# A Fourier filter and a two-layer network on one core: how the array between the two forward stages is laid out in DRAM, which loads come first, and one step more between a piece and its inverse pair

## The chip, the core and the metric

The kernel runs on one core of a Trainium2 chip. Its engines work side by side and wait for each other by semaphores: TensorE (PE in the profile; its weight loads are PEld) multiplies matrices, VectorE (DVE) and ScalarE (ACT) do element-wise work and empty the matrix accumulators in PSUM, GpSimd (POOL) and SyncE (SP) here mainly issue DMAs. [...] The metric is the device time of one execution in microseconds. Before the change three runs took 862.39, 861.15 and 859.33 us, median 861.15 us.

## The reference

```python
def _attn_ref(x, filt_r, filt_i):               # x: 8 x 3008 x 256
    X = np.fft.rfft(x, axis=1)
    F = (filt_r + 1j * filt_i)[None, :, :]      # 1505 x 256
    y = np.fft.irfft(X * F, n=x.shape[1], axis=1)
    return y.astype(np.float32)

def _moe_ref(x, w_in, w_out, alpha):            # x: 24064 x 256, w_in: 256 x 2048
    h = x @ w_in
    g = np.maximum(h, 0.0) + alpha * np.minimum(h, 0.0)
    return (g @ w_out).astype(np.float32)       # w_out: 2048 x 256
```

The first function's result, its 8 x 3008 rows taken as 24064 tokens, goes into the second. Arrays come and go in float32; the kernel works in fp16 with float32 accumulation.

## The kernel before

**The transform.** 3008 is 47 times 64. Each of the eight batches goes through four stages of small matrix products, called pieces here; a class `Fft` holds one batch.

- Stage A (`piece_a`, L162, 16 pieces): the 47-point transform. A piece is one product of 94 x 512 (L168) into a PSUM bank named psF, copied to `asb` by L250 (ACT) or L253 (DVE). Rows of `asb` are 96 = two halves h times 48 numbers k; along a row lie 32 values of s, each with 256 channels. `save_a` (L171) writes a quarter of `asb` to `a_dram`, after every fourth piece.
- `turn_a` (L175) reads `a_dram` back as `at`, with s on the partitions: the turn between the two forward stages. It can begin only when all four saves have landed.
- Stage B (`piece_b`, L184, 12 pieces): two products L188 into psF, then two DVE multiplications with the filter, uu (L191, by `filt_s`) and ww (L192, by `filts_s`). Batch 0 uses `piece_b0` (L195), with other banks.
- Stage C (`piece_c`, L211, 12 inverse pairs): four products, L220 (reads uu) and L221 (reads ww), into psF, copied to `v` by ACT. `turn_c` (L224) writes `v` to `v_dram` by quarters and, after the last, reads `v_dram` back as `zt` by quarters. Each read starts when the writes have landed.
- Stage D (`piece_d`, L238, 16 pieces): four small products L243 into psF, copied to `yT`, the input of the network.

**The network.** 48 blocks of tokens (`sizes`, L300: twelve for each pair of batches, the sixth of 384 tokens, the others of 512), of 16 steps each. Step j runs `up(j)` (L327): two products L332 into the bank pair `hps`; at an odd j the activation follows, ACT `gt` (L337), DVE `m` twice (L340) and an addition (L341). Then comes `down(j)` (L344) of the block before: four (three) products L350 into `op`, and at j = 7 and 15 (10 and 15 in a short one) a copy `osb` (L355, ACT) and its stores (L316).

**The order.** Nothing is rearranged by a scheduler: each engine executes its instructions as the Python code issues them. The prologue runs batch 0 through A, B and C and four D pieces. Then the steps are counted on, 0 to 767, and `plan` (L359 on) puts the pieces of batch b at given steps: after `up` and `down` of its step, a piece is issued. `plan_fft(b, a0, ga, ta, b0, gap, d0)` puts A piece i at step a0 + ga i, the turn at ta, B piece k at b0 + gap k, its inverse pair (C) three steps after it, and D from d0 on. Block 6 of each pair of batches (step 96 on) needs the D pieces of the odd batch.

**Banks.** psF has two banks for all pieces A, B, C and D. A piece may begin only when the copy (or, for B, the ww product) that empties its bank is done. Which bank a piece gets is decided when the program is built, so not strictly in turn.

**Queues.** SP issues saves, turns, `v_dram` and `zt`, constants and stores, strictly in order; a DMA that must wait holds up all behind it. POOL issues, also in order, what is converted from float32: x (`load_x`, L120, eight DMAs a batch), the filter (`load_filt`, L126), w_in (`win_s`) and w_out (`wout_s`). Each of the two has eight semaphores for its DMAs, so a ninth waits until the first has landed. Two small POOL copies into `gate` hold the queue: the first (L273) until `at` of batch 0 has landed, the second (L293) until `zt` of batch 0 has.

`filts_s`, the filter with its two halves exchanged, is made by two DMAs from `filt_s` (L291), issued after `zt` of batch 0; batch 1 is the first to read it. `xs` has four buffers, so a load of the next batch waits until the A pieces of the buffer's present contents are done.

Of the kernel before, what the change touches and what calls it, by code (L numbers as in the profile page):

```python
# [10 lines left out]
FP16 = mybir.dt.float16  # L11
# [5 lines left out]
NK1 = 24  # L17
D = 256
NB = 8
DFF = 2048  # L20
NH = 32
# [45 lines left out]
def kernel(  # L67
# [10 lines left out]
    nc = tc.nc  # L78
# [4 lines left out]
    twi_d = nc.inline_tensor(twi_np.astype(np.float16), name="c_twi")  # L83

    konst = ctx.enter_context(tc.tile_pool(name="konst", bufs=1))
# [7 lines left out]
    psO = ctx.enter_context(tc.tile_pool(name="psO", bufs=2, space=bass.MemoryType.PSUM))  # L93
    psF = ctx.enter_context(tc.tile_pool(name="psF", bufs=2, space=bass.MemoryType.PSUM))
    dram = ctx.enter_context(tc.tile_pool(name="dram", bufs=1, space=bass.MemoryType.DRAM))
    a_dram = dram.tile([NB, 96, NH, D], FP16, name="a_dram")
    v_dram = dram.tile([NB, 96, NH, D], FP16, name="v_dram")
    ctx.enter_context(tc.manual_schedule())

# [4 lines left out]
    twi_s = konst.tile([128, NK1, 2, 128], FP16, name="twi_s")  # L104
    filt_s = konst.tile([128, NK1, D], FP16, name="filt_s")
# [4 lines left out]
    alm_s = konst.tile([128, 16], FP32, name="alm_s")  # L110
    win_s = konst.tile([128, 2, DFF], FP16, name="win_s")
    wout_s = konst.tile([128, 16, D], FP16, name="wout_s")
    gate = konst.tile([128, 2], FP16, name="gate")
    yT = konst.tile([128, 2, 2 * NFFT], FP16, name="yT")

    def xrow(b, h, c):
        return bass.AP(tensor=x.tensor, offset=x.offset + (b * NFFT + NH * h + 8 * c) * D,
                       ap=[[N2 * D, N1], [1, 8 * D]])

    def load_x(b, c):  # L120
        xs = p_x.tile([2 * N1, 8 * D], FP16, name="xs")
        for h in range(2):
            nc.gpsimd.dma_start(out=xs[h * N1 : h * N1 + N1], in_=xrow(b, h, c))  # L123
        return xs

    def load_filt(dst, pbase, src, ka, kb):  # L126
        n = kb - ka
        nc.gpsimd.dma_start(
            out=dst[pbase : pbase + 32, ka:kb],
            in_=bass.AP(tensor=src.tensor, offset=src.offset + ka * D,  # L130
                        ap=[[47 * D, 32], [D, n], [1, D]]))
        nc.gpsimd.dma_start(
            out=dst[pbase + 32 : pbase + 64, ka:kb],
            in_=bass.AP(tensor=src.tensor, offset=src.offset + (N1 - ka) * D,
                        ap=[[47 * D, 32], [-D, n], [1, D]]))

    nc.sync.dma_start(out=wf1_s, in_=wf1_d.ap())
    xc = {(0, c): load_x(0, c) for c in range(4)}
    nc.sync.dma_start(out=al16, in_=moe_alpha.rearrange("(j p) -> j p", p=128))
    nc.sync.dma_start(out=twf_s[:, 0:12], in_=twf_d.ap()[:, 0:12])  # L140
    for ka, kb in ((0, 12), (12, 24)):
        load_filt(filt_s, 0, filt_r, ka, kb)
        load_filt(filt_s, 64, filt_i, ka, kb)
    make_identity(nc, id32)

    def bank(wide=False):
# [5 lines left out]
    class Fft:  # L152
# [16 lines left out]
            evict(self.asb[:, 2 * i : 2 * i + 2].rearrange("p a d -> p (a d)"), ps[0:96])  # L169

        def save_a(self, c):  # L171
            s = slice(8 * c, 8 * c + 8)
            nc.sync.dma_start(out=a_dram[self.b, :, s], in_=self.asb[:, s])

        def turn_a(self, eng, ka=0, kb=NK1):  # L175
            for h in range(2):
                for c in range(2):
                    r = h * 48 + c * NK1
                    q = c * 64 + NH * h
                    eng.dma_start(  # L180
                        out=self.at[q : q + NH, ka:kb],
                        in_=a_dram[self.b, r + ka : r + kb].rearrange("k s d -> s k d"))

        def piece_b(self, kp):  # L184
            px = bank().rearrange("p (k d) -> p k d", k=2)
# [69 lines left out]
    both = (on_act, on_dve)  # L255


    f0 = Fft(0)
# [2 lines left out]
        if i % 4 == 3:  # L261
            f0.save_a(i // 4)
    f0.turn_a(nc.sync, 0, 12)
    f0.turn_a(nc.scalar, 12, 24)
    nc.sync.dma_start(out=twi_s[:, 0:12], in_=twi_d.ap()[:, 0:12])
    nc.sync.dma_start(out=twf_s[:, 12:24], in_=twf_d.ap()[:, 12:24])
    nc.sync.dma_start(out=twi_s[:, 12:24], in_=twi_d.ap()[:, 12:24])
    nc.sync.dma_start(out=wi3_s, in_=wi3_d.ap())
# [1 line left out]
    nc.tensor.transpose(alp[:, 0, 0:16], al16, id32)  # L270
    nc.vector.tensor_copy(al_s, alp[:, 0, 0:16])
    nc.gpsimd.tensor_scalar(alm_s, al_s, 1.0, -1.0, OP.mult, OP.add)
    nc.gpsimd.tensor_copy(gate[:, 0:1], f0.at[:, 11, 0:1])  # L273
    for kt in range(2):
        nc.gpsimd.dma_start(out=win_s[:, kt], in_=moe_w_in[kt * 128 : (kt + 1) * 128])
    for q in range(2):
        nc.gpsimd.dma_start(
            out=wout_s[:, 8 * q : 8 * q + 8],
            in_=moe_w_out[1024 * q : 1024 * q + 1024].rearrange("(j p) d -> p j d", p=128))
# [10 lines left out]
        o = 64 * half  # L290
        nc.sync.dma_start(out=filts_s[o : o + 64], in_=filt_s[64 - o : 128 - o])  # L291

    nc.gpsimd.tensor_copy(gate[0:96, 1:2], f0.zt[:, 31, 0:1])  # L293
    for c in range(4):
        xc[(1, c)] = load_x(1, c)
    for i in range(4):
        f0.piece_d(i, both[i % 2], i % 2 == 1)

# [62 lines left out]
    def put(step, fn, *args):  # L361
        plan.setdefault(step, []).append((fn, args))

    def plan_fft(b, a0, ga, ta, b0, gap, d0):
        f = Fft(b)
        for i in range(16):
            put(a0 + ga * i, f.piece_a, i, on_act)
        for c in range(4):
            put(a0 + ga * (4 * c + 3), f.save_a, c)
            if b + 1 < NB:  # L370
                put(a0 + ga * (4 * c + 3) + 1,
                    lambda b=b, c=c: xc.update({(b + 1, c): load_x(b + 1, c)}))
        put(ta, f.turn_a, nc.sync)
        for kp in range(12):
            put(b0 + gap * kp, f.piece_b, kp)
            put(b0 + gap * kp + 3, f.piece_c, kp, on_act)
        for q in range(4):
            put(b0 + gap * (3 * q + 2) + 4, f.turn_c, q)
        for i in range(16):
            put(d0 + min(i, 4) + 2 * max(i - 4, 0), f.piece_d, i, on_act)  # L380

    for i in range(4, 16):
        put(i - 4, f0.piece_d, i, both[i % 2])
    plan_fft(1, 10, 1, 26, 40, 3, 92)
    plan_fft(2, 50, 2, 86, 104, 5, 187)
    for b in range(3, NB):
        p = 96 * (b - 1)
        plan_fft(b, p - 54, 2, p - 22, p + 6, 5, p + 91)

    prev = None  # L390
    step = 0
# [43 lines left out]
```

## Time and profile before

| What | Value |
|---|---|
| Median of three runs | 861.15 us (859.33 to 862.39) |
| Profiled execution: span | 861.4 us, 0.25 us over the median |
| PE busy | 799.4 us (93%) |
| DVE, ACT busy | 612.9 us (71%), 586.6 us (68%) |
| First A piece, first B piece of batch 0 | 7.5 us, 33.0 us |
| First D piece of batch 0, first `up` | 63.1 us, 64.6 us |
| B pieces of batch 1 begin (step 40) | 110.4 us |
| B pieces of batch 2 begin (step 104) | 186.6 us |
| PE busy from 200 to 680 us | 474.5 of 480 us |

The time that lies around the span is not shown apart: the profiled execution is given by its span alone, and it agrees with the runs to 0.03%.

The page's second part cuts the span into 40 slices of 21.5 us and shows, in tenths, how busy each engine was; its fourth part follows the chain of work that ended last back from the end; the timeline shows instructions in order of time, with the idle time before an instruction and what ended it in square brackets; the stretches view sums busy time by engine in stretches that one names. In the stretches view GB/s is what the DMA engines moved, counted at the writing side, and the DMA share can be over 1, since packets overlap.

### The profile page before, as it was taken

What the parts mean: (1) busy time and instruction counts of PE and PEld (TensorE: products, weight loads), DVE (VectorE), ACT (ScalarE), POOL (GpSimd) and SP (SyncE); (2) the same over time, 40 slices, a digit from 0 to 9 for tenths busy, and PEclk for the clock granted to TensorE, in tenths of its full rate; (3) what the DMA queues carried; (4) which work ended last, traced back from release to release, by engine and by line L of the source; (5) the groups of instructions that cost most, each with busy time, mean ns of one, the idle gap of its engine ahead of it and who ended that gap; (6) DMA issues with size and microseconds to landing.
All of it is one profiled execution on the core that took longest, in us unless ns stands there. A gap on an engine that the chain in (4) does not pass through costs nothing.

```text
span 861.4 us, 15404 instructions
## 1 busy us (share of the span) xinstructions
PE 799.4 (93%) x5809; PEld 541.7 (63%) x5809; DVE 612.9 (71%) x1361; ACT 586.6 (68%) x817; POOL 41.4 (5%) x85
## 2 busy tenths in 40 slices
PE   3458989979999999999999999999999999999997
PEld 1134556756666766676666766676666766676665
DVE  2246668758877787678877787778877788777773
ACT  2027757767787767777777767777777866677663
POOL 4103000000000000000000000000000000000000
PEclk9989989999999999999999999999999999999999
DMA  9989835761368224772268323682148122411111
GB/s 212 250 171 197 179 69 133 157 144 41 75 148 199 60 62 97 172 158 51 53 162 195 73 64 83 164 181 50 43 120 186 50 68 50 129 38 39 39 41 49
DMA packets 95378, 95.95 MB, mean 111 GB/s; under 512 B 8312, under 2 KB 85128, under 8 KB 95176
## 3 DMA queue, kind: packets, MB, share of 16 engines
q1 hardware_dynamic: 85448, 78.19, 35.8%
q0 software_dynamic: 8256, 16.00, 12.3%
q10 hardware_dynamic: 1600, 0.79, 0.5%
q8 instruction: 45, 0.74, 0.4%
q14 instruction: 29, 0.24, 0.1%
HBM read 59.55 MB, written 49.81 MB: 127 GB/s over the span
## 4 chain that ended last, share of the span: by engine, by line
PE 70%; DVE 13%; ACT 7%; DMA 6%; issue 2%; SPq 1%; POOL 0%; ACTq 0%; DVEq 0%; POOLq 0%
PE hps L332 29%; PE op L350 28%; ACT gt L337 6%; DVE gt L341 4%; DVE m L340 4%; PE psF L168 3%; DVE ww L192 3%; DVE uu L191 3%; PE psF L221 2%; DMA at<-a_dram 2%; PE psF L243 2%; DMA a_dram<-asb 2%; PE psF L220 1%; DMA xs<-in_x_dram 1%; PE psF L188 1%
## 5 line engine op out<-in xcount | busy, mean ns | idle before, releaser
L337 ACT ACTIVATE gt<-hps 128x1024 f16<-128x1024 f32 (+1 forms) x384 | 385.1, 1003 | 134.6 <-PE hps L332 134.1
L332 PE MATMUL hps<-yT,win_s 128*128 128x512 f16 (+1 forms) x1536 | 454.3, 377 | 1.1 <-ACT yT L250 1.0
L350 PE MATMUL op<-wout_s,gt 128*128 128x256 f16 x3008 | 453.3, 273 | 0.6 <-DVE gt L341 0.6
L350 PEld LDWEIGHTS <-gt 128*128 128x128 f16 x3008 | 294.4, 98 | 192.5 <-issue 2.8
L340 DVE TENSOR_SCALAR m<-gt,alm_s 128x512 f16<-128x512 f16 (+1 forms) x768 | 233.5, 346 | 164.1 <-ACT gt L337 162.8
L341 DVE TENSOR_TENSOR gt<-gt,m 128x1024 f16<-128x1024 f16 (+1 forms) x384 | 261.6, 681 | 24.3 <-DVE m L340 0.9
L332 PEld LDWEIGHTS <-win_s 128*128 128x128 f16 x1536 | 145.6, 98 | 31.6 <-issue 5.0
L250 ACT ACTIVATE asb<-psF 96x512 f16<-96x512 f32 x120 | 70.7, 593 | 40.2 <-PE psF L168 40.2
L250 ACT ACTIVATE v<-psF 128x512 f16<-128x512 f32 x84 | 50.2, 598 | 34.9 <-PE psF L221 34.9
L250 ACT ACTIVATE yT<-psF 128x376 f16<-128x376 f32 x120 | 58.1, 484 | 20.9 <-PE psF L243 20.7
L191 DVE TENSOR_TENSOR uu<-psF,filt_s 128x512 f16<-128x512 f32 x84 | 57.4, 683 | 6.7 <-PE psF L188 6.7
L355 ACT ACTIVATE osb<-op 128x512 f32<-128x512 f32 x96 | 56.3, 587 | 6.9 <-PE op L350 3.7
L168 PE MATMUL psF<-xs,wf_s 94*96 94x512 f16 x120 | 47.8, 398 | 11.0 <-DMA xs<-in_x_dram 8.3
L192 DVE TENSOR_TENSOR ww<-psF,filts_s 128x512 f16<-128x512 f32 x84 | 57.1, 679 | 0.0
L123 POOL DMA_DIRECT2D xs<-in_x_dram x64 | 32.9, 522 | 458.2 <-PE psF L168 457.1
L243 PE MATMUL psF<-wi_s,zt 96*128 96x94 f16 x504 | 42.7, 207 | 10.8 <-DMA zt<-v_dram 9.0
L243 PEld LDWEIGHTS <-zt 96*128 96x128 f16 x512 | 36.3, 100 | 18.9 <-DMA zt<-v_dram 9.3
L221 PE MATMUL psF<-ww,twi_s 128*128 128x256 f16 x168 | 41.1, 272 | 6.2 <-DVE ww L192 3.5
L220 PE MATMUL psF<-uu,twi_s 128*128 128x256 f16 x168 | 42.9, 272 | 1.1 <-ACT yT L250 0.5
L188 PE MATMUL psF<-at,twf_s 128*128 128x256 f16 x168 | 32.3, 274 | 8.1 <-issue 4.5
L220 PEld LDWEIGHTS <-twi_s 128*128 128x128 f16 x192 | 19.0, 99 | 18.0 <-issue 13.2
L250 ACT ACTIVATE v<-op 128x512 f16<-128x512 f32 x12 | 7.2, 597 | 32.4 <-PE op L221 32.4
(35 smaller groups left out, 130.8 us busy)
## 6 DMA issues: line engine op xcount, KB each, us to landing
out_dram<-osb SPq DMA_DIRECT2D x128, 128.0 KB
a_dram<-asb SPq DMA_DIRECT2D x32, 384.0 KB
v_dram<-v SPq DMA_DIRECT2D x128, 96.0 KB
zt<-v_dram SPq DMA_DIRECT2D x32, 384.0 KB
xs<-in_x_dram POOLq DMA_DIRECT2D x64, 188.0 KB, 5.1
at<-a_dram SPq DMA_DIRECT2D x28, 384.0 KB
twi_s<-c_twi SPq DMA_DIRECT2D x2, 768.0 KB
filts_s<-filt_s SPq DMA_DIRECT2D x2, 768.0 KB
```

The costliest lines, as they stand in the source:

```text
L168: nc.tensor.matmul(ps[0:96], wf1_s, xs[:, o : o + 512], start=True, stop=True)
L191: nc.vector.tensor_mul(uu, px, filt_s[:, 2 * kp : 2 * kp + 2])
L192: nc.vector.tensor_mul(ww, px, filts_s[:, 2 * kp : 2 * kp + 2])
L220: nc.tensor.matmul(pv[:, kh], twi_s[:, k1, 0], uu[:, kh], start=True, stop=False)
L221: nc.tensor.matmul(pv[:, kh], twi_s[:, k1, 1], ww[:, kh], start=False, stop=True)
L243: nc.tensor.matmul(ps[:, m], self.zt[:, 8 * g + 4 * mh + m, dh * 128 : dh * 128 + 128], wi3_s, start=True, stop=True)
L250: nc.scalar.activation(o, i, AF.Copy)
L332: nc.tensor.matmul(self.hps[:, j % 2, 0:tn], win_s[:, kt, j * 128 : (j + 1) * 128], yT[:, kt, self.t0 : self.t0 + tn], start=(kt == 0), st ...
L337: nc.scalar.activation(g[:, :, 0:tn], self.hps[:, :, 0:tn], AF.Copy)
L340: nc.vector.tensor_scalar(m[:, i, 0:tn], g[:, i, 0:tn], 0.0, a, OP.min, OP.mult)
L341: nc.vector.tensor_add(g[:, :, 0:tn], g[:, :, 0:tn], m[:, :, 0:tn])
L350: nc.tensor.matmul(self.op[:, si % 2], self.gts[k][:, 128 * si : 128 * si + 128], wout_s[:, k], start=(k == 0), stop=(k == 15))
```

## The change

Five things are changed.

1. `a_dram` is laid out as s, k, channel in place of k, s, channel. `save_a` writes it in two DMAs (one for each half h), each in pieces of 512 bytes with gaps; `turn_a` reads it in two DMAs (64 partitions each, one for each c) in place of four, each partition's share being contiguous (12 KB; 6 KB in each half of batch 0's turn).
2. In the prologue the first half of `twi_s` is loaded right after the first half of `twf_s`, in place of after the turn; the second half of the filter is loaded after the first `gate`, in place of before it; the second half of batch 0's turn is issued by SP in place of ACT.
3. The x of batch 1 is loaded ahead of w_out; the second `gate` is gone.
4. Batch 1's A pieces lie at steps 2 to 17 in place of 10 to 25 and are emptied by ACT and DVE in turn, in place of ACT alone; its turn is at 20 in place of 26, its B pieces at 32, 36, ... in place of 40, 43, ...; the turns of batches 3 to 7 are two steps later.
5. In all planned batches the inverse pair is four steps after its B piece in place of three, and `turn_c` follows one step later too.

```diff
-    a_dram = dram.tile([NB, 96, NH, D], FP16, name="a_dram")
+    a_dram = dram.tile([NB, 2 * NH, 2 * NK1, D], FP16, name="a_dram")
...
     nc.sync.dma_start(out=twf_s[:, 0:12], in_=twf_d.ap()[:, 0:12])
-    for ka, kb in ((0, 12), (12, 24)):
-        load_filt(filt_s, 0, filt_r, ka, kb)
-        load_filt(filt_s, 64, filt_i, ka, kb)
+    nc.sync.dma_start(out=twi_s[:, 0:12], in_=twi_d.ap()[:, 0:12])
+    load_filt(filt_s, 0, filt_r, 0, 12)
+    load_filt(filt_s, 64, filt_i, 0, 12)
...
         def save_a(self, c):
-            s = slice(8 * c, 8 * c + 8)
-            nc.sync.dma_start(out=a_dram[self.b, :, s], in_=self.asb[:, s])
+            for h in range(2):
+                r = NH * h + 8 * c
+                nc.sync.dma_start(
+                    out=a_dram[self.b, r : r + 8].rearrange("s k d -> k s d"),
+                    in_=self.asb[48 * h : 48 * h + 48, 8 * c : 8 * c + 8])
 
         def turn_a(self, eng, ka=0, kb=NK1):
-            for h in range(2):
-                for c in range(2):
-                    r = h * 48 + c * NK1
-                    q = c * 64 + NH * h
-                    eng.dma_start(
-                        out=self.at[q : q + NH, ka:kb],
-                        in_=a_dram[self.b, r + ka : r + kb].rearrange("k s d -> s k d"))
+            for c in range(2):
+                eng.dma_start(
+                    out=self.at[64 * c : 64 * c + 64, ka:kb],
+                    in_=a_dram[self.b, :, NK1 * c + ka : NK1 * c + kb])
...
     f0.turn_a(nc.sync, 0, 12)
-    f0.turn_a(nc.scalar, 12, 24)
-    nc.sync.dma_start(out=twi_s[:, 0:12], in_=twi_d.ap()[:, 0:12])
+    f0.turn_a(nc.sync, 12, 24)
...
-    nc.gpsimd.tensor_copy(gate[:, 0:1], f0.at[:, 11, 0:1])
+    nc.gpsimd.tensor_copy(gate, f0.at[:, 11, 0:1])
+    load_filt(filt_s, 0, filt_r, 12, 24)
+    load_filt(filt_s, 64, filt_i, 12, 24)
     for kt in range(2):
         nc.gpsimd.dma_start(out=win_s[:, kt], in_=moe_w_in[kt * 128 : (kt + 1) * 128])
+    for c in range(4):
+        xc[(1, c)] = load_x(1, c)
     for q in range(2):
         nc.gpsimd.dma_start(
             out=wout_s[:, 8 * q : 8 * q + 8],
...
-    nc.gpsimd.tensor_copy(gate[0:96, 1:2], f0.zt[:, 31, 0:1])
-    for c in range(4):
-        xc[(1, c)] = load_x(1, c)
...
-    def plan_fft(b, a0, ga, ta, b0, gap, d0):
+    def plan_fft(b, a0, ga, ta, b0, gap, d0, evicts=(on_act, on_act)):
         f = Fft(b)
         for i in range(16):
-            put(a0 + ga * i, f.piece_a, i, on_act)
+            put(a0 + ga * i, f.piece_a, i, evicts[i % 2])
...
-            put(b0 + gap * kp + 3, f.piece_c, kp, on_act)
+            put(b0 + gap * kp + 4, f.piece_c, kp, on_act)
         for q in range(4):
-            put(b0 + gap * (3 * q + 2) + 4, f.turn_c, q)
+            put(b0 + gap * (3 * q + 2) + 5, f.turn_c, q)
...
-    plan_fft(1, 10, 1, 26, 40, 3, 92)
+    plan_fft(1, 2, 1, 20, 32, 4, 92, both)
     plan_fft(2, 50, 2, 86, 104, 5, 187)
     for b in range(3, NB):
         p = 96 * (b - 1)
-        plan_fft(b, p - 54, 2, p - 22, p + 6, 5, p + 91)
+        plan_fft(b, p - 54, 2, p - 20, p + 6, 5, p + 91)
```

More of the change, by code (lines that the diff above doesn't have):

```diff
@@ L112 @@
     wout_s = konst.tile([128, 16, D], FP16, name="wout_s")
-    gate = konst.tile([128, 2], FP16, name="gate")
+    gate = konst.tile([128, 1], FP16, name="gate")
     yT = konst.tile([128, 2, 2 * NFFT], FP16, name="yT")
```

## The prediction

> **What bounds the kernel now.** I read the page's slices first, then stretches, the chain and the timeline of each hole.
>
> ```profile
> PE   3458989979999999999999999999999999999997
> DMA  9989835761368224772268323682148122411111
> ```
>
> From the tenth slice on TensorE is full; what can be won lies before 200 us and in small gaps. The DMA row is near full just where PE is not. Stretches (start and end, length, busy time of PE, PEld, DVE, ACT and POOL, the granted clock, DMA share, GB/s):
>
> ```profile
> 15.80:33.00 17.20, 0.00 (x0) 0.00 (x0) 0.00 (x0) 0.00 (x0) 0.20 (x1) 1.00 1.18 249
> 54.70:63.00 8.30, 0.00 (x0) 0.00 (x0) 0.00 (x0) 0.02 (x1) 0.00 (x0) 0.68 0.68 159
> 105.90:110.30 4.40, 0.00 (x0) 0.00 (x0) 1.07 (x3) 0.22 (x1) 0.00 (x0) 0.84 1.20 214
> 110.30:115.80 5.50, 5.43 (x20) 2.92 (x21) 2.60 (x5) 1.57 (x2) 0.00 (x0) 0.51 0.11 37
> 182.90:186.50 3.60, 0.03 (x1) 0.00 (x0) 1.18 (x3) 0.48 (x1) 0.00 (x0) 1.00 1.02 228
> 186.50:190.90 4.40, 4.35 (x22) 2.56 (x23) 2.60 (x5) 2.37 (x4) 0.00 (x0) 0.61 0.01 4
> ```
>
> Four holes: the turn of batch 0, its way from C to D, the turns of batches 1 and 2. Behind the last two the clock is half for 5.4 and 3.4 us, so each costs half of that again. The chain names the DMAs of the first two:
>
> ```profile
> 15.74 6.18 DMA a_dram<-asb
> 23.40 9.52 DMA at<-a_dram
> 56.08 2.00 DMA v_dram<-v
> 58.20 4.83 DMA zt<-v_dram
> ```
>
> Two places of the timeline carry the rest: a D piece of batch 0 that waits for the DVE copy behind the activation, and an inverse pair that waits for ww.
>
> ```profile
> 71.01 1.02 ACT L337 ACTIVATE gt<-hps 128x1024 f16<-128x1024 f32 x1
> 72.07 0.62 DVE L340 TENSOR_SCALAR m<-gt,alm_s 128x512 f16<-128x512 f16 x2 [0.20 <-ACT gt L337]
> 72.72 0.69 DVE L341 TENSOR_TENSOR gt<-gt,m 128x1024 f16<-128x1024 f16 x1
> 73.33 0.54 DVE L253 CAST yT<-psF 128x376 f16<-128x376 f32 x1
> 73.92 0.33 PE L243 MATMUL psF<-wi_s,zt 96*128 96x94 f16 x4 [0.34 <-DVE yT L253]
> ...
> 217.36 0.68 DVE L192 TENSOR_TENSOR ww<-psF,filts_s 128x512 f16<-128x512 f32 x1
> 217.50 0.27 PE L220 MATMUL psF<-uu,twi_s 128*128 128x256 f16 x1
> 218.09 0.27 PE L221 MATMUL psF<-ww,twi_s 128*128 128x256 f16 x1 [0.32 <-DVE ww L192]
> ```
>
> **Part 1, batch 0 up to its first B piece (33.0 us).** From 2.6 us on the DMA engines are never free, so bytes count. Rates from stretches: x 211 GB/s (6 to 8 us), w_in and w_out 207 (38 to 42), scattered reads of a turn 193 (178 to 184), scattered 512-byte writes of `v_dram` 282 (48 to 50), long contiguous reads 333 to 432 (32 to 36). Ahead of the first B piece there is less: half the filter, 0.79 MB at 143 to 250 GB/s, 4.4 us; half the turn, with the other half now contiguous, 7.2 us (24 to 33 us less latency) become 2.1. There is more: 0.79 MB of `twi_s`, 2.1 us, and the saves' 1.57 MB at 282 GB/s in place of 332 or more (16 to 18 us): 0.9 at least, I take 1.5. Four more SP issues of 0.5 us hide between the A pieces, but the last, which delays the turn. Latency, covered by the queue before, adds 1.5. Sum -4.4 -5.1 +2.1 +1.5 +1.5 = -4.4: first B at about 29 (27.5 to 31; scattered writes as slow as scattered reads give +2.5). The turn's second half, moved from ACT to SP, is issued 1 us later and is needed 12 us later; nothing.
>
> The filter's second half, behind the first gate, must land before B piece 6 (12.6 us after the first: 45.6 against 33.05). Four issues of 0.6 us and 4.4 us of transfer beside 3 us of `twf_s` and `twi_s` put it at 9.5: covered.
>
> **Part 2, from C to D (63.1 us).** Behind the gate POOL now has 0.79 MB of filter, 1.05 of w_in, 1.54 of x, 1.05 of w_out: 4.4 + 5 + 7.3 + 5.2 = 22 us; SP has 2.1 + 2.9 us of turn and constants and 5.6 of `v_dram`. From 29.5 that fills the engines to 61 or 62. Before, all had landed at 50 and the last write and the `zt` read ran alone: 54.7 to 58.1 and 58.2 to 63.0. How long they take beside other loads the trace shows in part: the first quarter of v, beside w_out, took 7.9 us from its first issue at 41.87 to 49.8, the last 3.3. C ends 21.7 us after the first B: 50.7. Then v 3.3 to 7.9, I take 6.8; `zt` 4.8 to 8.5, I take 6.8, since w_out runs out meanwhile. D begins at 64.4 (59 to 68): 1.3 us lost where 4.4 were won.
>
> **Part 3, D and A together.** x of batch 1 is there now: its wait (76.7 us, 0.9) goes. But steps 2 to 11 hold a D and an A piece each. By the program's waits, one psF bank then serves only D, the other only A, and at odd steps both are emptied by DVE, behind m, m and the addition of the same step. Before, a D piece waited for a DVE copy three steps old. Now, from the start of an activation: 1.02 to its end, 0.62 m, 0.69 addition, 0.54 yT, D starts at +2.91 (71.01 to 73.92 above), `asb` 0.69, A starts at +3.55; A, up and ACT's copy of A (0.38 + 0.59) bring the next activation at +4.45. Two steps thus take 4.45 us, where activations stood 2.0 apart (68.76 to 74.72: three pairs in 6.0). Following it through: activation of step 3 at 6.7 after the first D, of step 11 at 24.5, then 8.2 to step 18, at 32.7. With 14 steps of 0.87 step 32 is reached after 45.0 us; before, after 34.8 (97.9 less 63.1), A pieces until step 25 included. Loss 10.2 (6 to 13). PE is busy only 1.6 of 4.45 us; should its clock fall, each pair costs 0.6 more, up to 2.7 in all; I take 0.8, since windows at 60% stayed fast and one at 25% did not.
>
> [...]
>
> **Part 4, the turn of batch 1.** The last save is issued 35.5 to 36.3 us after the first D, lands 2 later; two issues, 1.15 of latency, 1.57 MB at 333 to 432 GB/s: `at` lands at about 44 and is wanted at 45.9. The hole (4.65 by start times) and its slow clock (half of 5.4) go: 7.3 won (4 if x of batch 2 slows the read by 3). `filts_s` (7.4 us behind `zt`) is long there.
>
> **Part 5, B and C of batch 1.** With a gap of four steps C, B and A of batch 2 meet in steps 52 to 76, seven times; A waits 0.63 for the copy of v, as four times before (and 0.34 once): 1.5 lost.
>
> **Part 6, batch 2's turn and batch 1's D.** `turn_c` of the last quarter is at step 81, not 77, and stands on SP behind three stores (2.35 us) and the two saves of step 80. From the start of step 80: stores to 3.7, saves to 4.6, v to 6.5, landed at 8.8, `zt` 4.9 later (163.86 to 168.83 before): 13.7. D is wanted at 10.65. A new wait of 3.1 (1.5 to 5) with 1.6 of slow clock (0 to 1.7). The old hole at step 104 (3.8 and 1.7) is covered, as the turn is issued right behind `zt` and lands 4 us early. Won: 0.8 (-2 to +4).
>
> **Part 7, the inverse pairs.** From batch 2 on, six pairs of a batch start L221 late (0.59 from L220, not 0.11, above) or L220 late: by start times 13.5 us in all, 0.25 to 0.57 each. ww ends 0.5 too late; a step is 0.87, so all go. New waits, from the program's banks: a B behind a D whose copy stands behind gt and osb on ACT (0.43) and an A behind a pair in a step with osb (0.5), in five or six batches: 4.6. Won 8.9 (5 to 11). The two-step shift of later turns costs nothing: they have 26 steps; SP waits less.
>
> [...]
>
> **Sum.** -1.3 -10.2 -0.8 +7.3 -1.5 +0.8 +8.9 = 3.2 us won: 858.2 by the profiled span of 861.4, which is 0.25 over the median; so 858.0.
>
> **Rivals.**
> - The front is early: x and w_out leave `v_dram` and `zt` their old times. For it: `v` at 51 to 54 us ran 3.3 just behind w_out. Against: the 7.9. D at 59 in place of 64.4: 853.
> - Slower, by the banks: the pairs' waits only move to whichever piece next wants the bank, so that the old 13.5 stay. For it: L168 already waited for v (2.0 us, five times). Against: banks named by the program give 4.6. Then 867; it is slower than before from 3 us won or less.
> - Slower, by the front: first B at 31 and contended times in full, D at 69.1 and later quarters of `zt` holding D pieces 2 us more: 865; slower from a D start past 70.3.
> - The change does nothing where D meets A, DVE's copies being hidden: 848. Against: that chain has no slack in it.
>
> **Numbers.** 0.3% is 2.6 us, about what can be told from no change. The forecast has 0.45 (853.5 to 862, half of it faster, half same), the early front 0.2, banks 0.13, late front 0.17, hidden copies 0.05. Faster 0.46, same 0.22, slower 0.32. Range 849 to 868.
>
> **What would show it.** First B near 29; first D near 64, w_out still moving at 58; activations 4.4 us apart in steps 3 to 11; no wait before batch 1's first B; one of 3 us before batch 1's first D in place of batch 2's first B; L221 no longer waiting for ww. Wrong it would be made by banks that free earlier than I follow, or by 512-byte writes at another rate.

## The result, and the profile after

The changed kernel takes 873.3 us (870.6 to 873.7), the kernel before 860.2 beside it (859.3 to 862.4): 1.0132 of it, with a 95% interval of 1.0104 to 1.016. It is slower, by 9 to 14 us; the forecast was 858, within 849 to 868. The profiled execution has a span of 871.9 us, 10.5 more than that of before (861.4). All sums below are between these two executions. (A run's time is 1.8 us more than its span, 873.68 against 871.9; so the profiled execution of before lay about 2 us above its median and not at it, and the medians differ by 13.1.)

The slices of the changed kernel first, with the granted clock and the DMA engines:

```profile
PE   3525779889999999999999999999999999999997
PEclk9966689999999999999999999999999999999999
DMA  9998441666247721674257522783237413411111
```

From the tenth slice on nothing is lost. Before that PE has its dips where it had them, but broader: the third slice (44 to 65 us) has fallen from 5 to 2, and three slices in a row show a clock of 6 tenths. The stretches say what fills them (columns as before: start and end, length, busy time of PE, PEld, DVE, ACT and POOL, clock, DMA share, GB/s):

```profile
17.70:30.50 12.80, 0.00 (x0) 0.00 (x0) 0.06 (x1) 0.00 (x0) 0.19 (x1) 1.00 0.88 209
50.30:69.50 19.20, 0.00 (x0) 0.00 (x0) 0.00 (x0) 0.11 (x1) 0.00 (x0) 0.51 1.03 196
74.70:81.40 6.70, 3.78 (x27) 1.89 (x25) 4.14 (x9) 3.65 (x6) 0.00 (x0) 1.00 0.73 157
81.50:101.80 20.30, 14.01 (x51) 5.97 (x50) 10.11 (x23) 8.17 (x13) 3.10 (x6) 0.50 0.41 78
118.00:123.70 5.70, 0.00 (x1) 0.00 (x0) 1.10 (x3) 0.25 (x1) 0.00 (x0) 0.89 0.81 194
123.70:130.50 6.80, 6.78 (x30) 3.96 (x31) 3.37 (x8) 2.05 (x2) 0.00 (x0) 0.59 0.01 2
193.00:196.50 3.50, 0.25 (x6) 0.20 (x6) 0.84 (x3) 0.00 (x0) 0.00 (x0) 1.00 0.97 227
```

The turn of batch 0 now ends at 30.5 in place of 33.0, but the way from C to D takes more than 19 us in place of 9: no engine works, and the DMA engines are full at 196 GB/s. In the steps behind it, D and A of batch 1 together, the clock is whole from 74.7 to 81.4 us and half from 81.5 to 101.8. The turn of batch 1 still has its hole (5.7 us, then 6.8 at a clock of 0.59). Batch 2's has gone, and a wait of D for `zt` stands at 193 in its place. The chain names the front's links:

```profile
2.86 8.35 DMA xs<-in_x_dram
...
18.09 5.75 DMA a_dram<-asb
24.63 5.77 DMA at<-a_dram
...
44.02 15.31 DMA v_dram<-v
59.35 5.76 DMA v_dram<-v
65.24 4.25 DMA zt<-v_dram
```

The link that ends at 11.2 is x's second chunk, whose first A piece starts at 11.35 in place of 9.28; the first chunk's starts at 7.85 in place of 7.54. From 44 to 65 `v_dram` holds the chain. The timeline of one odd step in which D and A meet, and of the activation after it:

```profile
80.72 1.01 ACT L337 ACTIVATE gt<-hps 128x1024 f16<-128x1024 f32 x1
81.77 0.66 DVE L340 TENSOR_SCALAR m<-gt,alm_s 128x512 f16<-128x512 f16 x2 [2.00 <-ACT gt L337]
82.45 0.69 DVE L341 TENSOR_TENSOR gt<-gt,m 128x1024 f16<-128x1024 f16 x1
83.06 0.54 DVE L253 CAST yT<-psF 128x376 f16<-128x376 f32 x1
83.66 0.47 PE L243 MATMUL psF<-wi_s,zt 96*128 96x94 f16 x4 [1.87 <-DVE yT L253]
84.25 0.59 PE L168 MATMUL psF<-xs,wf_s 94*96 94x512 f16 x1
85.73 1.02 ACT L337 ACTIVATE gt<-hps 128x1024 f16<-128x1024 f32 x1 [0.26 <-PE hps L332]
```

D starts 2.94 us behind the activation and A 3.53 behind it, as the prediction followed it (2.91, 3.55); the next activation comes after 5.01, not 4.45, as PE's own matmuls run at half the clock (0.50) from 81.5 us on. An inverse pair, from the same view, runs without its wait:

```profile
237.56 0.68 DVE L192 TENSOR_TENSOR ww<-psF,filts_s 128x512 f16<-128x512 f32 x1
238.52 0.27 PE L220 MATMUL psF<-uu,twi_s 128*128 128x256 f16 x1
238.63 0.27 PE L221 MATMUL psF<-ww,twi_s 128*128 128x256 f16 x1
```

By the start times of the steps, the 10.5 us come about like this (waits that the text gives are counted in this way too, which makes them 0.15 to 0.2 us longer than the idle time that the profile shows in brackets):

| | before | after | won (+) |
|---|---|---|---|
| first B piece | 33.05 | 30.54 | (+2.5, part of the next row) |
| first D piece | 63.1 | 69.5 | -6.4 |
| from there to step 32 | 34.8 | 47.4 | -12.6 |
| step 32 to step 96 | 76.0 | 84.0 | -7.9 |
| step 96 to step 112 | 21.0 | 15.2 | +5.8 |
| step 112 to step 760 | 646.8 | 636.0 | +10.8 |
| span | 861.4 | 871.9 | -10.5 |

### The profile page after: what moved, and what is told of

Read it like the earlier page. It is cut to its first block, busy times and chain, and to the rows that moved or that the text cites. A ratio compares the mean times of both kernels' runs of the same rounds, so it can differ in the third digit from the quotient of the medians.

```text
span 871.9 us, 15422 instructions
## 1 busy us (share of the span) xinstructions
PE 800.1 (92%) x5809; PEld 544.6 (62%) x5809; DVE 619.3 (71%) x1369; ACT 584.9 (67%) x809; POOL 41.1 (5%) x84
## 4 chain that ended last, share of the span: by engine, by line
PE 84%; DMA 8%; ACT 3%; DVE 2%; issue 1%; SPq 1%; POOL 0%; ACTq 0%; DVEq 0%; POOLq 0%
PE hps L332 35%; PE op L350 35%; PE psF L168 3%; DMA v_dram<-v 3%; PE psF L243 2%; PE psF L188 2%; PE psF L221 2%; DMA at<-a_dram 2%; PE psF L220 2%; DMA zt<-v_dram 1%; ACT gt L337 1%; DMA a_dram<-asb 1%; DMA xs<-in_x_dram 1%; ACT v L250 1%; ACT osb L355 1%
## 5 line engine op out<-in xcount | busy, mean ns | idle before, releaser
L250 ACT ACTIVATE asb<-psF 96x512 f16<-96x512 f32 x112 | 66.3, 592 | 47.8 <-PE psF L168 47.8
L168 PE MATMUL psF<-xs,wf_s 94*96 94x512 f16 x120 | 49.8, 415 | 16.3 <-DMA xs<-in_x_dram 9.4
L168 PEld LDWEIGHTS <-wf_s 94*96 94x96 f16 x128 | 17.0, 137 | 15.8 <-issue 14.6
```

The lines of the kernel that those rows point to most:

```text
L168: nc.tensor.matmul(ps[0:96], wf1_s, xs[:, o : o + 512], start=True, stop=True)
L250: nc.scalar.activation(o, i, AF.Copy)
```

## The experiments

After the result I had three theories of what was lost, and they do not exclude each other: (a) POOL's early loads keep the DMA engines from `v_dram` and `zt` of batch 0; (b) D and A of batch 1 sharing steps; (c) something holds the turn of batch 1, although its read is contiguous. The rival to all of them is that the new layout itself costs more than it brings.

**w_out behind zt.**

```diff
-    for q in range(2):
-        nc.gpsimd.dma_start(
-            out=wout_s[:, 8 * q : 8 * q + 8],
...
         nc.sync.dma_start(out=filts_s[o : o + 64], in_=filt_s[64 - o : 128 - o])
+    nc.gpsimd.tensor_copy(gate[0:96, 1:2], f0.zt[:, 31, 0:1])
+    for q in range(2):
+        nc.gpsimd.dma_start(
+            out=wout_s[:, 8 * q : 8 * q + 8],
...
```

> After, with one move: the load of w_out waits for zt of batch 0 (as x of batch 1 did in before), so that only w_in and x of batch 1 run beside v_dram. Theory (POOL's loads beside v_dram and zt make the first D late): w_out's 2048 packets ran from 52.4 to 63.9 us, all of it beside the last quarters of v_dram; without them the last landing of v_dram is 2 to 4 us sooner, first D at 66 to 67.5 in place of 69.5, time 870 to 871. Rival (what holds v_dram is only SP's own order of issues, or x of batch 1): first D stays at 69 to 69.5, time 873. Second rival: first D comes at 63 as in before, then w_out was all of it and the time is 867.

Measured: 867.4 us, 1.0061 of before (1.0035 to 1.0087). First D at 63.8, where the second rival had put it. The chain's last two links of the front are now

```profile
57.67 1.97 DMA v_dram<-v
59.77 3.97 DMA zt<-v_dram
```

in place of 59.35 5.76 and 65.24 4.25. Theory (a) holds, and more simply than I had it: 1.05 MB of w_out, at the 207 GB/s that the prediction read for it, are 5.1 us of all sixteen DMA engines, and D comes 5.7 sooner. What stands between C and D is the time for the bytes still to move.

**Batch 1's plan put back.**

```diff
-    plan_fft(1, 2, 1, 20, 32, 4, 92, both)
+    plan_fft(1, 10, 1, 26, 40, 3, 92)
```

> After, with the plan of batch 1 put back: A pieces from step 10 on ACT alone, turn at 26, B from step 40 with a gap of 3, C four steps behind B. Theory (D and A sharing steps 2 to 11 cost 12.7 us, and the turn of batch 1 still waits): from the first D to step 32 takes 35 us and not 47.5 (-12.7), the wait of 5.9 with its slow clock at step 32 goes (-9.4), a hole like that of before comes at step 40 (+7.4 to +8), the triple pieces go (-1.5), zt of batch 1 is issued 3 steps sooner, so its wait at step 92 shrinks (-2 to -5), and the hole of batch 2's turn comes back by 0 to 5. Sum about -15: 858 (855 to 862). Rival (the slow clock and the loads at the front cost the time, not the shared steps): 866 to 870, first D to step 32 still above 42.

Measured: 860.1 us, 0.9971 of before (0.9951 to 0.999); span 857.3. First D is as late as in after (70.0), yet step 32 comes 34.6 us later, not 47.4, so the 12.8 us of (b) are gone. A hole of 5.4 appears at step 40 for the one of 5.9 at step 32, and batch 2's wait is back with 2.6. Theory (b) holds with its size.

**The pairs alone.**

```diff
-            put(b0 + gap * kp + 3, f.piece_c, kp, on_act)
+            put(b0 + gap * kp + 3 + late, f.piece_c, kp, on_act)
-            put(b0 + gap * (3 * q + 2) + 4, f.turn_c, q)
+            put(b0 + gap * (3 * q + 2) + 4 + late, f.turn_c, q)
```

on the kernel before, with `late` 1 for batches 2 to 7 and 0 for batch 1.

> Before, with one part of the change alone: for batches 2 to 7, C four steps behind B and v five behind its last C (batch 1 and the front as before). Theory (the pairs' gain of 8.9 us stands by itself): 851.5 (850 to 853.5), L221 no longer waiting for ww, waits of 4 to 5 us by the banks in their place. Rival (the gain was bound to the other parts, the two later steps of the turns above all, or new waits eat it here): 857 to 860.

Measured: 849.1 us, 0.9856 of before (0.9817 to 0.9896), a little better than the theory. Step 112 to step 760 takes 635.9 us, as in after (636.0), against 646.8: 10.9 us stand by themselves. Another 2.7 lie between steps 104 and 112 (10.3 in place of 13.1 us).

**The layout alone**, on the kernel before: `save_a`, `turn_a` and the shape of `a_dram` as in after, nothing else.

> Before, with one part alone: a_dram written scattered in eight DMAs per batch and read contiguous in two. Theory (batch 0 gains, as the turn's first half needs 2 us in place of 7, the saves cost 1.5 more; batch 1's turn stays bound by x of batch 2 that runs beside it at 200 to 218 GB/s in both traces): first B at 29.5 to 30.5 in place of 33.0, first D 2.5 to 3.5 us sooner, the hole at step 40 as long as before within 1.5 us; time 857 (855.5 to 859). Rival (the layout only moves the bytes' cost from the read to the write): first B at 32 to 33, time 860. Rival (the scattered saves beside the stores of the output and x make batch 1's and 2's turns late): 862 to 865.

Measured: 866.1 us, 1.0051 of before (1.0032 to 1.0071). First C at 39.2 in place of 35.7. The chain:

```profile
15.62 3.83 SPq L174
19.50 6.54 DMA a_dram<-asb
26.76 9.62 DMA at<-a_dram
```

The saves are done 4.1 us later (26.0 against 21.9), and the turn, now contiguous, takes 9.6 us, no less than the scattered one of before (23.40 9.52). The hole at step 40 grew from 4.65 to 6.1. The layout by itself is a loss; the last rival comes nearest, but puts it all on the later batches.

**The layout undone, all else as in after.**

> After, with the layout of a_dram put back (contiguous saves, scattered reads; the turn's second half stays on SP). Theory (the layout moves the cost from the read to the write and gains nothing, as it did alone: first C 3.5 us later): first C at 31 to 33.5 in place of 33.2, first D at 67 to 69.5, held by w_out all the same; the wait at step 32 within 1.5 us of the 5.9; time 868 to 873. Rival (the layout brought what the prediction gave it, 3.6 us at batch 0 and the short turn of batch 1): first C at 36 to 37, the wait at step 32 at 9 or more, time 876 to 880.

Measured: 867.5 us, 1.0067 of before (1.0046 to 1.0087), so 0.0065 of before better than after. First B at 28.5, first D at 67.8, the wait at step 32 at 3.1. The part of the change that was to speed up the turn slows it. Why shows in the stretches in which the turn of batch 1 is read: the changed kernel,

```profile
113.55:121.42 7.87, 4.45 (x32) 2.78 (x29) 4.30 (x10) 3.27 (x4) 0.00 (x0) 1.00 1.00 211
```

and this one, with reads of 512 bytes each:

```profile
108.52:116.63 8.11, 6.10 (x43) 3.99 (x41) 5.52 (x13) 4.21 (x5) 0.00 (x0) 1.00 1.19 199
```

The contiguous read moves its 1.57 MB hardly faster (7.9 against 8.1 us), with nothing of weight beside it. By the trace its 12 KB packets take 0.97 us each (median), 202 GB/s for sixteen engines, while the 6 KB packets of `twi_s` take 0.23 in before, 420 GB/s, and the 3 KB packets of `twf_s` 0.12, 406 GB/s. All are long and contiguous, so length is not the cause.

**The first half of twi_s behind the turn**, as in before.

> After, with the first half of twi_s behind the turn of batch 0 again, as in before. Theory (its 6 KB packets made the first x chunk land at 11.2 and not 7.4; but the first D is held by w_out and x of batch 1, so little of it reaches the end): first A at 7.5, first B 1.5 to 2.5 us sooner (28 to 29), first D 0 to 1.5 us sooner, time 871.5 to 873.5. Rival (the 3.8 us go through to D): D at 65.7 to 67, time 869 to 870. Rival (twi_s now comes late for C): first C at 33 or later all the same.

Measured: 870.2 us, 1.0103 of before (1.0069 to 1.0138). First A at 6.9, first B 2.1 us sooner (28.45), but then C waits 2.6 us for `twi_s` (first C at 33.5), and the first D comes only 0.4 us sooner. The theory's moments and its second rival are both right: at the front a byte that is moved back comes due later. (The 11.2 of the expectation is x's second chunk, not its first; its first A piece starts 2.1 us sooner here, at 9.27.) The time lies just below the theory's: the span is 3.5 us shorter, most of it at step 32 (a wait of 3.8, not 5.9), though the intervals of the two ratios overlap.

**x of batch 2 behind the turn of batch 1.**

```diff
+            def late_x():
+                nc.gpsimd.tensor_copy(gate[:, 1:2], f.at[:, 23, 0:1])
+                for c in range(4):
+                    xc[(2, c)] = load_x(2, c)
+            put(ta + 1, late_x)
```

> After, with one load moved: x of batch 2 (1.5 MB in the middle of the saves and the turn of batch 1, 107 to 122 us) waits until at of batch 1 is there. Theory (the turn of batch 1 is slow because x of batch 2 shares the DMA engines with it, 200 to 218 GB/s for both): at lands 3 to 5 us sooner, the wait of 5.9 at step 32 falls to 1 to 2.5 and the slow clock behind it with it; A of batch 2 has 18 steps left for its x; time 865 to 868. Rival (the last save lands too late, and the read takes its 8 to 9 us by its own): the wait stays above 4.5 us, time 872 to 874. Rival (x of batch 2 comes late in turn): PE waits at step 50, 870 or more.

Measured: 870.7 us, 1.0098 of before (1.0067 to 1.0129). The theory fell. The turn's packets run from 113.5 to 121.2, in after from 113.55 to 121.42: x of batch 2 had ended at 109.5, ahead of them, and the expectation had misread that. The wait at step 32 is nevertheless 3.5 and not 5.9: in after the turn's last completion came 2.2 us behind its last packet, here 0.8, and also 0.8 with the later `twi_s`. In these traces a DMA of the turn ends with sixteen signals. In after fifteen of the last one's had come by 122.1, 0.7 behind the last packet, and the sixteenth came at 123.7; here all sixteen had come by 122.0. Why one signal came late stays open, and with it why some 2 us (and their clock) of the wait at step 32 vary.

**The turn into 128 partitions.** Left was what distinguishes the two kinds of long packets: the constants go into 128 partitions, each DMA of the turn into 64. In the kernel before, the copies into `filts_s` are of that second kind, and their 12 KB packets took 0.95 us as well (65.2 to 74.4 us).

```diff
+    twf = twf.reshape(2, 64, NK1, 128).transpose(1, 0, 2, 3).reshape(128, NK1, 128).copy()
-            for c in range(2):
-                eng.dma_start(
-                    out=self.at[64 * c : 64 * c + 64, ka:kb],
-                    in_=a_dram[self.b, :, NK1 * c + ka : NK1 * c + kb])
+            eng.dma_start(
+                out=self.at[:, ka:kb],
+                in_=a_dram[self.b].rearrange("s (c k) d -> (s c) k d", c=2)[:, ka:kb])
```

> After, with each turn as one DMA into all 128 partitions in place of two into 64: at holds the two column halves in neighbouring partitions (2s and 2s+1), the rows of the constant twf are reordered to match, and a_dram is then read as 128 rows of 12 KB one behind the other. Same bytes, same packets. Theory (a transfer into 64 partitions runs at half rate: in after the 12 KB packets of batch 1's turn took 0.97 us each, 202 GB/s for 16 engines, with nothing beside them, the 6 KB packets of twf_s and twi_s, into 128 partitions, 0.23, 420 GB/s): 12 KB packets of 0.47 to 0.55 us, the turn of batch 1 read in 4 to 4.5 us in place of 7.9, the wait at step 32 at 1.5 to 2.5 in place of 5.9 with less slow clock behind it; first B 1 to 2 us sooner; first D still at 68.5 to 69.5; time 866 (864 to 868.5). [...] Rival (the source sets the rate, DRAM that was just written): packets stay at 0.9 or more, the wait at 5 to 6, time 872 to 874.

Measured: 862.6 us, 1.0014 of before (0.9998 to 1.0031): more than the theory forecast, 10.7 us below after. Same bytes, same packets, and the read of batch 1's turn lasts 5.7 us in place of 7.9. Its first 4.3 us, ahead of the stores that then run beside it:

```profile
109.10:113.40 4.30, 4.30 (x32) 2.90 (x30) 3.18 (x8) 2.28 (x3) 0.00 (x0) 1.00 1.00 319
```

The median packet takes 0.47 us; the whole read gains less than that, 7.9 to 5.7, as some packets take longer. The wait at step 32 is 0.5 and the slow clock behind it is gone; first B comes at 28.7 and first D at 65.4, 4.1 us sooner, which is again about what 1.57 MB at 400 in place of 200 GB/s give back (3.9). Theory (c) has its cause in the partitions that a DMA writes: the traces have 202 to 211 GB/s for 64 partitions and up to 420 for 128, and of the same bytes a 12 KB packet took 0.97 us into 64 and 0.47 into 128. It is not the count of DMAs: in after the two halves came one after the other (signals of the first from 118.07 to 118.55, of the second from 121.75), so that one DMA into 64 partitions had the engines to itself. That DRAM is now read without gaps could matter too, but `filts_s` reads no DRAM and is as slow into 64 (0.95 us). Why a packet takes twice as long there, no run shows.

**Towards a kernel that beats both.** First the pairs alone, the filter's second half behind the first gate, and w_out behind `zt` and x of batch 1.

> Before, with C four steps behind B in batches 2 to 7 (849.1 by itself), the filter's second half behind the first gate as in after, and w_out behind zt, after x of batch 1. Layout, twi_s and batch 1's plan as in before. Theory (what runs beside the turn, v_dram and zt of batch 0 sets the front): the 4.4 us of filter leave the front, first B at 29 to 30.5, first D at 58.5 to 60.5 in place of 62.4, the rest as in the kernel with the pairs alone; time 845 (843 to 847.5). Rival (w_out and x of batch 1, both behind zt, come late): PE waits at steps 10 to 20 for more than 2 us, time 848 to 852. Rival (the filter's second half beside twi_s, twf_s and the turn's second half holds B): first D not before 62, 849.

Measured: 850.4 us, 0.9874 of before (0.9842 to 0.9907). First D at 58.6 as expected, but PE then waits for w_out at step 16:

```profile
81.43 0.60 PE L351 MATMUL op<-wout_s,gt 128*128 128x256 f16 x4 [2.55 <-DMA wout_s<-in_moe_w_out_dram]
```

By step 26 (93.6; 93.5 with the pairs alone) nothing of the 3.8 us is left. The rival named the mechanism and, with 848 to 852 us, the time. x was issued at 63.9, and its first packet moved at 68.9, behind the copies into `filts_s`.

> The combined kernel with three moves at the front: the gate ahead of x of batch 1 opens at zt's second quarter and not its fourth, w_out comes behind the first chunk of x and ahead of the other three, and the copy into filts_s (12 KB packets into 64 partitions, 61.7 to 69.9 us, which held the first x packet from its issue at 63.9 until 68.9) is issued at step 12. Layout as in before. Theory: first D stays at 58.5, x of batch 1 and w_out land 5 us sooner, the wait of 2.7 for w_out at step 16 and that of 1.5 for x at step 10 go, with the slow clock behind them: 5 to 6 us off the combined kernel's span, 845 (842.5 to 847). Rival (x and w_out now hold the later quarters of zt, which D waits for): PE waits at steps 0 to 8 for 2 us or more, 848 to 850.

Measured: 851.6 us, 0.9891 of before (0.986 to 0.9922). The theory fell on one of its moves: at step 12 nothing on SP holds the copies into `filts_s`, so they went out at 57.7, right behind `zt`, as before, and x's first packet came at 68.5. With w_out now ahead of x's second chunk, PE waits 2.8 us for that chunk at its first use (step 14; the expectation further on says 13).

> The kernel with the earlier front, and besides it a_dram written scattered and read in one DMA into 128 partitions. Theory (read that way the layout is worth having): the wait at step 40 (4.4 and its slow clock of half of 5.5) falls to 1.5 or less, first B 0 to 2 us sooner; 5 to 8 us off the kernel with the earlier front, 838.5 (835 to 842). Rival (the scattered saves cost at the front what the read gains there, as the layout alone cost 3.5 us at first C): first C 2 to 3.5 us later, 842 to 846.

Measured: 840.9 us (840.2 to 844.1), 0.9777 of before (0.9744 to 0.9809): faster than both, and within the forecast. Its slices:

```profile
PE   3657989999999999999999999999999999999997
```

First B at 28.0, first D at 55.2 (59.9 without the layout), the wait at step 40 2.7 in place of 4.2 (1.5 or less was expected), batch 2's wait gone. Read into 128 partitions, the layout is worth 12 us of span (838.8 against 850.7), where into 64 it cost time. What is left beside that 2.7 is the wait for x's second chunk:

```profile
76.14 0.63 PE L168 MATMUL psF<-xs,wf_s 94*96 94x512 f16 x1 [2.66 <-DMA xs<-in_x_dram]
```

> The kernel with the earlier front and the one-DMA turn, and two moves: the copies into filts_s stand on SP behind batch 1's first save (step 13), which does wait, where at step 12 nothing on SP held them and they went out right behind zt, at 53 us; and B, C and v of batch 1 come two steps later (B from step 42). Theory (filts_s's 12 KB packets into 64 partitions, 57.8 to 66.5 us, held the first x packet of batch 1 from its issue at 57 until 63.8, and so x's second chunk until PE waited 2.8 for it at step 13; the wait of 2.7 at step 40 is 3 steps of 0.87): x starts to move by 60, the wait at step 13 goes with its slow clock (about 4 us), the wait at step 42 is 1 or less (about 2 to 3 us with its clock), zt of batch 1 lands 0 to 0.6 us too late for its D: span 832 (829.5 to 835) from 838.8, median 834. Rival (x does not start sooner, something else than filts_s holds POOL's packets back): the wait at step 13 stays above 2, 837 to 839.

Measured: 843.2 us, 0.9786 of before (0.9756 to 0.9817), no better. The theory is right about x: its first packet moves at 58.8, 1.3 us behind the issue, that wait is gone and step 40 comes 5.6 us sooner. But `filts_s` now stands in front of the later saves on SP:

```profile
75.11 1.95 SPq L385 DMA_DIRECT2D filts_s<-filt_s  x2
77.88 8.66 SPq L174 DMA_DIRECT2D a_dram<-asb  x4
```

Four issues that take 1.7 us in the kernel before it take 8.7, the turn comes late, and PE waits 5.6 us at step 42 (plus 2.1 for `zt` at step 92 and 1.4 for the turn of batch 2). So the copy cost PE 2.8 us in the first place and more in the second (why an issue behind it takes so long no run shows); the kernel of 840.9 us stays the best.

## Why the prediction was wrong

- **The step that failed** is the rate of the contiguous turn, in Part 1 ("7.2 us become 2.1") and Part 4 ("1.57 MB at 333 to 432 GB/s: `at` lands at about 44"). The rate was read at 32 to 36 us, where constants go into 128 partitions; the turn goes into 64 and moved at 200 to 211. What the prediction said could make it wrong were the banks and the rate of the 512-byte writes, not the rate of the read. The right row was in the trace of before: `filts_s`, 64 partitions, packets of 12 KB, 0.95 us. With the turn into 128 partitions the forecasts of three parts come out: first B at 28.7 (29 forecast), first D at 65.4 (64.4), no wait ahead of batch 1's first B (0.5). The whole read is still slower than the row: 5.7 us, where 333 to 432 GB/s make 3.6 to 4.7.
- **Part 1** gained 2.5 us in place of 4.4. The rate alone accounts for the rest: 28.7 with the turn into 128 partitions, where -4.4 makes 28.65. The 2.1 us for `twi_s` held, as the run that put it back showed (28.45 against 30.54).
- **Part 2** was to lose 1.3 and lost 6.4; D at 69.5 lies past the bound of 68. The sum treated `v_dram` and `zt` as durations, contended or not. The runs show that the DMA engines' time is what adds up: 1.05 MB of w_out taken away gives 5.7 us, a turn into 128 partitions 4.1.
- **Part 3** was to lose 11.0 with its clock and lost 12.6; the run with batch 1's old plan won 12.8 back. The chain of copies was right to 0.03 us. Short was the clock, half from 81.5 to 101.8 us: step 32 came 47.4 us behind the first D, 2.4 more than the 45.0 of the sum without it, where I had taken 0.8 out of a possible 2.7. The reading behind that, windows at 60% that stay fast, was too generous: from 74.7 to 81.4 us PE was busy for 56%, and then the clock fell to 0.50; in before the stretch from 180.6 to 184.0 us, behind which the clock stayed at 1.00 until 187.4, had 69%.
- **Part 4** was to win 7.3 and lost about 1.3: a hole of 5.9 and 2.8 of slow clock against 4.65 and 2.7. This is the largest miss, 8.6 us. The lower bound of a win of 4 was too narrow; it covered x of batch 2 beside the read, which turned out not to be there.
- **Parts 5 and 6** held: seven waits of 0.63; 3.4 us for `zt` ahead of batch 1's first D (3.1 forecast) and 1.7 of clock, and batch 2's hole gone.
- **Part 7** was to win 8.9 (5 to 11) and won 10.8 in after and 10.9 alone, all of it where it was expected.
- **The rivals.** The late front (first B at 31, D at 69.1) is what happened, at 30.5 and 69.5; its 865 still counted 7.3 for Part 4. The banks did not matter.
- **The two halves.** The prediction counted a DMA for each half of the partitions as one more issue and no more: 0.5 us each for the saves (Part 1), two issues for the turn of batch 1 (Part 4). For the turns, one DMA into all 128 partitions in place of two into 64 was worth 10.7 us.

The two largest misses, Parts 4 and 2 (8.6 and 5.1 us), make up the distance between the 3.2 us to be won and the 10.5 lost; what the other parts missed cancels out.

## What to carry to other kernels

Take the rate of a DMA from a row with the same count of partitions, not only the same length of packet: a contiguous read into 64 partitions was hardly faster here than a scattered one (7.9 against 8.1 us), and into all 128 its packets took half as long (0.47 against 0.97 us); reordering the rows of a constant made that possible without one instruction more. Where the DMA engines were full, a load ahead of a wait cost its full transfer time there (w_out, 5.1 us of transfer: D came 5.7 sooner without it), so ask of each load at which step it is first needed, and whether its queue will really hold it until then. A change of several parts is worth undoing part by part: the gain of the pairs alone (12 us) was larger than the whole change's loss let one guess.

## What was not expected of the hardware

- With the number of partitions that the turn's DMA writes, its rate changed: 12 KB packets took 0.97 us into 64 partitions and 0.47 into 128, from the same rows of `a_dram`.
- POOL's loads were slow whatever their partitions: packets of 4 KB took 0.32 us, 203 GB/s, both for w_in (128 partitions) and for x (47), where the 4 KB packets of SP's contiguous saves (96 partitions) took 0.16 to 0.17. But these loads convert: for 4 KB of fp16 written they read 8 KB of float32, which makes 406 GB/s on the reading side, near the 420 of the constants. No run separates the queue from the conversion, so the cause stays open.
- Scattered writes of 512 bytes into `a_dram` took 0.027 us each, 303 GB/s; scattered reads of 512 bytes into 32 partitions 0.048, 171 GB/s.
- SP issued in order, and a copy in its queue that waited for nothing left at once, however late its place in the program: with the earlier front, the copies planned for step 12 left ahead of step 0, at 57.7 us, right behind `zt`.
